# A Fourier filter and an MLP-mixer block on one core: weight loads held back for a moment, and the second group's inputs also in the filter's buffers

## The chip, the core and the metric

The kernel runs on one core of a Trainium2 chip. The core has a matmul engine (TensorE, "PE" in the profile, with its weight loads shown apart as "PEld"), VectorE ("DVE"), ScalarE ("ACT"), GpSimd ("POOL") and SyncE ("SP"). Each engine takes its own instructions strictly in the order in which the program lists them, and waits where one of them needs something that another engine or a transfer has not yet delivered. Three of them also issue DMAs: SP, ACT and POOL. A DMA behind a waiting instruction on its queue is not issued before that instruction is through. The metric is the device time of one execution in microseconds (us).

## The reference, cut to what matters

```python
X = np.fft.rfft(x, axis=1)                       # x: (8, 3008, 256) float32
Y = X * (filt_r + 1j * filt_i)[None]             # filters: (1505, 256)
y = np.fft.irfft(Y, n=3008, axis=1).astype(np.float32)

xt = y.transpose(0, 2, 1)                        # (8, 256, 3008)
h = np.maximum(xt @ w_tok1, 0) @ w_tok2          # 3008 -> 256 -> 3008 along the tokens
u = y + h.transpose(0, 2, 1)
h2 = np.maximum(u @ w_ch1, 0) @ w_ch2            # 256 -> 1536 -> 256 along the channels
out = (u + h2).astype(np.float32)
```

The weights of the mixer come in as 64-bit floats.

## The kernel before

**The filter.** The transform of length 3008 = 47 x 64 is done in steps. `a_unit` (line 462) multiplies one input tile of 2 token rows by a 64-point table; a batch has 12 units. For batches 1 to 7 ScalarE copies the result to a `t1` tile and stores it to DRAM (`z_tmp`). `b_unit` and `bi_unit` (lines 518 and 542) then go over 32 values of k: load the rows of `z_tmp`, multiply by a table, multiply by the filter on VectorE, multiply back, and store to DRAM (`g_tmp`). `t4_load` (line 594) reads `g_tmp` back in another layout. The filter rows lie in three tiles `filts`, cleared once at the start (line 924), and refilled in turn by `filt_load`, whose DMAs leave the padding rows alone. Batches go through the filter in the groups (0), (1, 2), (3, 4), (5, 6), (7).

**The inputs.** `x_load` (line 442) puts one unit, 256 KB in two DMAs, into a tile. Batch 0 uses six tile pools that are not needed yet. All later batches have the pool `xp` with XB = 2 tiles, loaded through SP: a new load can begin when the matmul on the tile before it has been done. `dft` is a generator: each `yield` is a place where the caller can put other work.

**The mixer.** `token_sums` (line 599) multiplies 24 token rows by `w1`, 96 matmul instructions (an fp32 product is two of them). `u_unit` and `u_quarter` multiply by `w2` and add the filtered input. `mix` (line 832) runs over items: 8 batches x 6 blocks of 512 tokens x 6 pairs of channel tiles, so 36 items a batch. One item is `up_first`, a ScalarE copy and two VectorE steps (`up_middle`), `up_last`, and the `down` products of the item before. Its places are numbered in the order 3, 0, 1, 2, and at each the main loop may advance the filter of the next group. For the second group (batches 1 and 2, during the items of batch 0) it advances at every place while there are `a_unit`s left (`spread`), and then 35 times over 48 places 1 and 2, that is over 24 items; for later groups at place 1 alone. The `t4` loads of batch 1 are emitted when that filter has ended, and `token_sums(1)` stands in item 32 of batch 0.

**The weights.** 38 tiles of 64-bit weights are brought to fp32. A tile has four steps, each a `yield`: its DMA (`begin`), one ScalarE activation on line 261 (`copy`), two VectorE operations on lines 263 and 264 (`middle`), and two on lines 267 and 269 (`end`). Tiles 0 to 11 are `w1`, 12 to 25 are `w2` (seven for each half; tiles 18 and 25 have 188 columns, the others 471), 26 to 37 the channel weights. Where the halves are added: for `w1` and the first BY_PE = 8 tiles of `w2` TensorE adds them (lines 302 and 303) and ScalarE copies the sum (line 305); for the rest VectorE adds them (line 291). For channel weights GpSimd then forms sums (`combine`, line 353). `convert` is `middle` and then `end` of the next tile in each iterator's turn, and after each `end` `copies` and `fill` let the next activation and the next DMAs go: a DMA is begun up to five tiles ahead of the last ended one, four among the last ten. Tiles 12 to 37 load through POOL.

**The prologue.** Lines 922 to 974: batch 0 goes through the filter (33 values of k, of which the last only finishes) while 16 tiles are converted, one half of a conversion at each k. At the last k a `middle` is called too, so from there on `middle` is one tile ahead of `end`. The rows of `g_tmp` are read back in four parts; the last one, 16 partitions, follows the last store. Then come the loads of the first two inputs of the second group, ten conversions with `token_sums(0)` after the one of tile 19, two more with the two `u_unit`s, and two `a_unit`s. All `w2` tiles are needed by the first `u_unit`, since each holds some of every block's columns. The ten remaining tiles are converted in the first five items, two in each, by half conversions (`late_half`, line 843).

Of the kernel before, what the change touches and what calls it, by code (L numbers as in the profile page):

```python
# [30 lines left out]
TC4 = 4  # L31
FB = 3
XB = 2
KC = 2
WC = 2
DT = 256
# [8 lines left out]
NG = 10  # L45
W2G = -(-N2 // NG)
PARTS = (0, 64, 96, 112)
BY_PE = 8
IN_B = 16
EARLY = 12  # L50
GROUPS = ((0,), (1, 2), (3, 4), (5, 6), (7,))
# [75 lines left out]
def kernel(  # L127
# [297 lines left out]
            advance(copy)  # L425
            copied[0] += 1

    begun = [0]

    def fill(ahead):  # L430
        while begun[0] < len(tiles) and begun[0] < ended[0] + (4 if begun[0] >= len(tiles) - len(LAST) else ahead):
            start()

    def start():
# [2 lines left out]

    xs = {}  # L440

    def x_load(b, c):

        where, tag = ((xp, "x"), (tp, "t"), (vp, "v"), (up, "u"), (t1p, "t1"), (t2p, "t2"))[c // 2] if b == 0 else (xp, "x")
        xc, dc = (2 * XC, D // 2) if b == 0 else (XC, D)
        d0, c = divmod(c, A // xc)
        t = where.tile([P, xc, dc], FP32, tag=tag, name="x")
        rows = x[b].rearrange("(n2 n1) d -> n2 n1 d", n1=N1)[:, :, ds(d0 * dc, dc)]
        for h in range(2):
            n = xc - 1 if h and (c + 1) * xc == A else xc  # L450
            lo = h * A + c * xc
            q = nc.gpsimd if b == 0 and h else nc.sync
            q.dma_start(t[h * HALF:(h + 1) * HALF, 0:n, :], rows[:, lo:lo + n, :])
            if n < xc:

                q.dma_start(t[h * HALF:(h + 1) * HALF, n:xc, :], rows[:, lo:lo + 1, :])
        xs[b, c + d0 * (A // xc)] = t
# [15 lines left out]
    def dft(bs):  # L473
# [13 lines left out]
            table_load(c)  # L487
            filt_load(c, first)

        ahead = NXC if first else XB  # L490
        for u in todo[0:ahead]:
            x_load(*u)
        if not first:
            yield True
        for i, u in enumerate(todo):
            if first and i in (0, 2):
                w_load(i // 2)
            if first and i in (6, 8):
                table_load(i // 2 - 1)
            a_unit(*u)  # L500
            if i + ahead < len(todo):
                x_load(*todo[i + ahead])
            yield i + 1 < len(todo)
            if first and (i + 1) % (NXC // 2) == 0:

                for d in range(i // (NXC // 2) * P, (i + 1) // (NXC // 2) * P, 16):
                    v = turned.rearrange("p s d -> p d s")[:, d:d + 16, :]
                    nc.vector.transpose(v, v)
# [33 lines left out]
        def bi_unit(k):  # L542
# [14 lines left out]
            if r == KC - 1:  # L557
                t3 = t3s.pop(c)
                for i, b in enumerate(bs):
                    nc.scalar.dma_start(g_d[b, ts(c, KC)].rearrange("k r d -> r k d"), t3[:, :, i, :])  # L560

        for c in range(2):
            t2_load(c)
            if not first:
                w_load(c)
# [25 lines left out]

    t4 = {}

    def t4_load(b, c, lo=PARTS[0], hi=P):
        if lo == 0:
            t4[b, c] = t4p.tile([P, TC4, D], FP32, tag="t4", name="t4")
        nc.sync.dma_start(t4[b, c][lo:hi], rows_of(g_d, b)[lo:hi, ts(c, TC4), :])

    def token_sums(b):
        acc = bank(free_bank()).rearrange("p (t d) -> p t d", t=TC)  # L600
# [231 lines left out]
    def mix(next_ready):  # L832

        wait = []
        pos, hhs, tts = {}, {}, {}

        def loads(b):
            if b + 1 < B and next_ready(b):
                for c in wait:
                    t4_load(b + 1, c)  # L840
                wait.clear()

        def late_half(f):
            if ended[0] < len(tiles):
                f()


        own = ({(3, 2): 0, (4, 2): 1}, {(2, 2): 0, (3, 0): 1, (3, 2): 2, (4, 0): 3})
        new = {(JP - 3, 2): 0, (JP - 2, 0): 1, (JP - 2, 2): 2, (JP - 1, 0): 3}

        def u_parts(b, m, jp, place):
            parts = own[b > 0] if m + 1 < MT else new if b + 1 < B else {}
            part = parts.get((jp, place))
            if part is None:
                return
            b, m = (b, m + 1) if m + 1 < MT else (b + 1, 0)
            u_part(b, m, part)
            if part == len(parts) - 1:
                if m:
                    wait.append(m)  # L860
                todo_v.extend(v_steps(b, m))
                if b and (b, m) < (B - 1, MT - 2):
                    w2m_load((m + 2) % MT)

        to_dram = [f for m in range(MT) for f in w2_sums(m)]
        items = [(b, m, jp) for b in range(B) for m in range(MT) for jp in range(JP)]
        n = MT * JP
        for i in range(len(items) + 1):
            now, old = i < len(items), i >= 1
            if now:  # L870
                b, m, jp = items[i]
                if i % n == 0:
                    wait.append(0)
                w = width(m)
                hhs[i] = hp.tile([P, 4, 256], FP32, tag="hh", name="hh")
                g = [bank("pg").rearrange("p (s n) -> p s n", s=2) for _ in range(2)]
                s = up_first(jp, uts[b, m], vts[b, m], w, g)
                up_middle(hhs[i], w, g, s)
                late_half(convert_middle)
                yield b, i % n, 3  # L880
            one_step()
            if old:
                bo, mo, jo = items[i - 1]
                tts[i - 1] = tp.tile([P, 4, 256], FP32, tag="t", name="t")
                for f in h_sums(hhs[i - 1], tts[i - 1], width(mo)):
                    f()
                down(mo, jo, 0, hhs[i - 1], tts[i - 1], pos.setdefault((bo, mo), []))
            if now:
                u_parts(b, m, jp, 0)
            late_half(convert_end)  # L890
            yield b, i % n, 0
            late_half(convert_middle)
            if now:
                up_last(jp, uts[b, m], vts[b, m], w, g, s, hhs[i])
            late_half(convert_end)
            one_step()
            loads(b)
            yield b, i % n, 1
            if old:
                down(mo, jo, 1, hhs.pop(i - 1), tts.pop(i - 1), pos[bo, mo])  # L900
                if jo == JP - 1:
                    todo_v.extend(finish(bo, mo, uts[bo, mo], pos[bo, mo]))
                    one_step()
                    one_step()
            if now:
                if b + 1 < B and i % n == n - 4:
                    h1s[b + 1] = token_relu(b + 1, token_sums(b + 1))
                u_parts(b, m, jp, 2)
                if jp == JP - 1:
                    while todo_v and m + 1 == MT:  # L910
                        one_step()
                if i >= 8 and to_dram:
                    to_dram.pop(0)()
                if i in (28, 29):
                    w2m_load(i - 28)
            loads(b)
            yield b, i % n, 2
        while todo_v:
            one_step()

    with tc.manual_schedule():
# [6 lines left out]
        for i, _ in enumerate(dft(GROUPS[0])):  # L928
            if i == 0:
                nc.scalar.dma_start(wai_t, wait_d)  # L930
            k = i - NXC - 2

            if i < NXC:
                if i in (1, 3, 5, 7, 9):
                    start()
                if i == NXC - 1:
                    copies()
                    for t, src in ((wa, wa_d), (wai, wai_d), (ident, ident_d)):
                        nc.scalar.dma_start(t, src)
            elif k >= 0:  # L940
                while half < 2 * IN_B * (k + 1) // K2:
                    if half % 2:
                        convert_end()
                    else:
                        convert_middle()
                    half += 1

                if 19 <= k < 25:
                    t4_load(0, k - 19, 0, PARTS[1])
                elif 26 <= k < 29:  # L950
                    for c in range(2):
                        t4_load(0, 2 * (k - 26) + c, PARTS[1], PARTS[2])
                elif k in (30, 31):
                    for c in range(3):
                        t4_load(0, 3 * (k - 30) + c, PARTS[2], PARTS[3])
        for c in range(A // TC4):
            t4_load(0, c, PARTS[3], P)
        both = wcp.tile([P, 2, JP, 7, P], FP32, tag="wc", name="wc")

        chan.extend((both[:, 0], both[:, 1]))  # L960
# [1 line left out]
        for i in range(IN_B, A // 2 + TC * W2G):  # L962
            convert()
            if i == A // 2 + BY_PE - 1:
                sum_up()
                acc = token_sums(0)
        h1s[0] = token_relu(0, acc)
        for dh in range(DH):
            convert()
# [13 lines left out]
        for b, i, place in mix(next_ready):  # L983
# [6 lines left out]
            due = place == 1  # L990
            if group == 0:
                due = spread
                if not spread and place in (1, 2):
                    at += 1
                    due = at * left // places > (at - 1) * left // places or at > places
            if due and not done:
# [32 lines left out]
```

## Time and profile before

| | |
|---|---|
| time, median of 5 runs | 2584.14 us (2576.14 to 2587.73) |
| the profiled execution's own time | 2586.17 us |
| its span | 2584.4 us |
| PE busy | 2495.0 us (97%) |
| PEld busy | 2052.2 us (79%) |
| DVE busy | 1912.8 us (74%) |
| ACT busy | 680.9 us (26%) |
| POOL busy | 575.8 us (22%) |
| moved by DMA | 248.37 MB, mean 96 GB/s |
| `token_sums(0)` begins | 124.9 us |
| first `u_unit` begins | 146.4 us |
| first item's ScalarE copy (line 729) | 154.8 us |
| the second group's last `a_unit` | 232.7 us |
| `token_sums(1)` begins | 495.9 us |

The profile is of one execution, and its spans are counted from the first instruction. Where an engine waits, the profile names what ended the wait; the chain of waits goes back from the last instruction to whatever released it, step by step. PE's busy time counts a matmul from its start to its modelled end, so neighbouring matmuls overlap, and a busy PE may still run below its peak rate.

### The profile page before, as it was taken

The numbers are of one execution on the slowest core, as the hardware profiler recorded it, in microseconds if no ns is written. First come the engines' busy times: TensorE is split into PE (matmuls) and PEld (weight loads), VectorE is DVE, ScalarE is ACT, GpSimd is POOL, SyncE is SP. The second block draws the span as 40 slices with busy tenths as digits, with TensorE's granted clock in tenths as the row PEclk, the third lists the DMA queues.
The fourth block names the chain that finished last, engine by engine and source line by source line (L and its number), as shares of the span: only waits on it lengthen the run. The fifth ranks groups of instructions, "written<-read, shape, count | busy, mean of one in ns | idle before, by whom it ended". The sixth has DMA issues, their size and how long they took to land.

```text
span 2584.4 us, 32295 instructions
## 1 busy us (share of the span) xinstructions
PE 2495.0 (97%) x11212; PEld 2052.2 (79%) x11212; DVE 1912.8 (74%) x3591; ACT 680.9 (26%) x1345; POOL 575.8 (22%) x1055
## 2 busy tenths in 40 slices
PE   6879999999999999999999999999999999999998
PEld 3556666888888777898888777798888888898887
DVE  6667888576686998756676899856788587757776
ACT  5623222123221222212221222212222122212222
POOL 5542232311211112112121111121121121211222
PEclk9999999999999999999999999999999999999999
DMA  9964344323342333213333333213333222111100
GB/s 216 233 186 149 116 127 146 96 93 104 103 124 78 97 104 82 92 48 103 119 109 90 89 100 112 85 37 103 102 95 107 63 79 71 39 31 36 44 13 20
DMA packets 166816, 248.37 MB, mean 96 GB/s; under 512 B 35300, under 2 KB 112474, under 8 KB 166654
## 3 DMA queue, kind: packets, MB, share of 16 engines
q1 hardware_dynamic: 94062, 152.01, 19.8%
q0 software_dynamic: 32640, 46.70, 7.3%
q10 hardware_dynamic: 39952, 47.61, 5.8%
q8 instruction: 89, 1.46, 0.2%
q14 instruction: 73, 0.60, 0.1%
HBM read 168.96 MB, written 77.22 MB: 95 GB/s over the span
## 4 chain that ended last, share of the span: by engine, by line
PE 74%; DVE 15%; DMA 5%; issue 2%; ACT 2%; POOL 0%; SPq 0%; ACTq 0%; DVEq 0%; POOLq 0%
PE ps_po L760 25%; PE ps_pg L726 15%; PE ps_pg L742 11%; PE ps_acc L603 3%; PE ps_b L603 3%; DVE t L704 3%; DVE hh L704 3%; PE ps_b L647 2%; PE ps_acc L647 2%; DVE u L704 2%; DVE s L704 2%; PE ps_b L625 2%; DMA x<-in_x_dram 2%; PE ps_acc L625 2%; PE ps_acc L524 1%
## 5 line engine op out<-in xcount | busy, mean ns | idle before, releaser
L805 POOL DMA_DIRECT2D out_dram<-r x757 | 410.5, 551 | 1778.1 <-ACT t L555 735.7
L704 DVE TENSOR_TENSOR hh<-ps_pg,s 128x512 f32<-128x512 f32 (+3 forms) x864 | 482.8, 586 | 368.4 <-ACT s L729 349.8
L747 ACT ACTIVATE hh<-hh 128x512 f32<-128x512 f32 (+1 forms) x576 | 347.8, 621 | 1191.4 <-DVE hh L704 1191.4
L760 PE MATMUL ps_po<-t,wc 128*128 128x256 f32 (+1 forms) x2304 | 537.5, 376 | 7.3 <-DVE t L704 6.4
L760 PEld LDWEIGHTS ps_po<-t,wc 128*128 128x128 f32 x2304 | 435.1, 190 | 132.3 <-issue 52.5
L726 PE MATMUL ps_pg<-v,wc 128*128 128x256 f32 (+1 forms) x1728 | 413.5, 375 | 2.4 <-DVE v L704 2.4
L760 PE MATMUL ps_po<-hh,wc 128*128 128x256 f32 (+1 forms) x1728 | 413.7, 376 | 0.2 <-ACT hh L747 0.2
L726 PEld LDWEIGHTS ps_pg<-v,wc 128*128 128x128 f32 x1728 | 327.9, 190 | 42.6 <-DVE v L704 5.5
L760 PEld LDWEIGHTS ps_po<-hh,wc 128*128 128x128 f32 x1728 | 328.9, 190 | 40.6 <-issue 2.2
L742 PE MATMUL ps_pg<-u,wc 128*128 128x256 f32 (+1 forms) x1152 | 293.9, 378 | 3.5 <-DVE hh L704 3.5
L704 DVE TENSOR_TENSOR t<-t,hh 128x256 f32<-128x256 f32 (+1 forms) x576 | 244.7, 425 | 19.9
L742 PEld LDWEIGHTS ps_pg<-u,wc 128*128 128x128 f32 x1152 | 217.0, 190 | 38.1 <-DVE hh L704 10.8
L704 DVE TENSOR_TENSOR s<-ps_pg,hh 128x512 f32<-128x512 f32 (+1 forms) x288 | 196.0, 681 | 30.7 <-DVE hh L704 0.9
L704 DVE TENSOR_TENSOR t<-hh 128x512 f32<-128x512 f32 (+1 forms) x288 | 192.3, 668 | 0.6 <-ACT hh L747 0.6
L729 ACT COPY s<-ps_pg 128x256 f32<-128x256 f32 (+1 forms) x288 | 106.0, 368 | 315.9 <-PE ps_pg L726 305.2
L742 PE MATMUL ps_pg<-v,wc 128*128 128x256 f32 (+1 forms) x576 | 169.2, 375 | 0.0
L726 PE MATMUL ps_pg<-u,wc 128*128 128x256 f32 (+1 forms) x576 | 169.2, 375 | 0.0
L726 PEld LDWEIGHTS ps_pg<-u,wc 128*128 128x128 f32 x576 | 109.5, 190 | 23.6 <-issue 11.3
L742 PEld LDWEIGHTS ps_pg<-v,wc 128*128 128x128 f32 x576 | 109.0, 190 | 13.2
L704 DVE TENSOR_TENSOR u<-ps_b,u 128x512 f32<-128x512 f32 (+3 forms) x105 | 61.1, 582 | 76.8 <-PE ps_b L647 60.3
L704 DVE TENSOR_TENSOR u<-ps_acc,u 128x256 f32<-128x256 f32 (+3 forms) x105 | 59.4, 566 | 61.3 <-PE ps_acc L647 42.4
L603 PE MATMUL ps_acc<-t,w 128*128 128x256 f32 x384 | 83.7, 380 | 1.1 <-ACT t L555 1.1
(125 smaller groups left out, 2532.0 us busy)
## 6 DMA issues: line engine op xcount, KB each, us to landing
w<-w_tmp SPq DMA_DIRECT2D x35, 896.0 KB
g_tmp<-t ACTq DMA_DIRECT2D x128, 192.0 KB
out_dram<-r POOLq DMA_DIRECT2D x698, 32.0 KB, 1.8
x<-in_x_dram SPq DMA_DIRECT2D x173, 128.0 KB
z_tmp<-t ACTq DMA_DIRECT2D x84, 256.0 KB
t<-z_tmp SPq DMA_DIRECT2D x112, 192.0 KB
t<-g_tmp SPq DMA_DIRECT2D x42, 512.0 KB
wb<-wbi_t SPq DMA_DIRECT2D x80, 224.0 KB
```

The lines of the kernel that those rows point to most:

```text
L524: nc.tensor.matmul(ps, wbs[k // WC][0:P if first else KR, k % WC, 0:P], t2, start=True, stop=True)
L603: nc.tensor.matmul(acc[:, t, :], w1[:, a, ts(t, P)], t4[b, a // TC4][:, a % TC4, :], start=(a == 0 and t == 0), stop=(a == A - 1 and t == ...
L625: nc.tensor.matmul(ps[:, ds(q * P, n)], t4[b, c][:, r, ts(dh, P)], wai[:, 0:n], start=(first and q == 0), stop=(not first and q == 3))
L647: nc.tensor.matmul(ps[:, ds(j * hw, hw)], h1[:, n, :], w2m[m % 2][:, at, 0:hw], start=(i < 2 and j == 0), stop=(j == len(todo) - 1))
L704: nc.vector.tensor_tensor(out=out, in0=in0, in1=in1, op=op)
L726: nc.tensor.matmul(ps[:, 0:hw], chan[0][:, jp, n, :], mov, start=True, stop=True)
L729: nc.scalar.copy(out=s[:, 0], in_=g[0][:, 0, 0:hw])
L742: nc.tensor.matmul(ps[:, 0:hw], chan[0][:, jp, n, :], mov, start=True, stop=True)
L747: nc.scalar.activation(out=hs, in_=hs, func=AF.Relu)
L760: nc.tensor.matmul(po[i][:, j, 0:hw], chan[1][:, jp, n, :], mov, start=(jp == 0 and first == 1), stop=(jp == JP - 1 and last == 1))
L805: q.dma_start(rows[g, e, :, ds(h * A + 4 * m, n)], blocks[ts(g, CW), h, e, 0:n])
```

## The change

The prologue and the first items are rearranged.

1. From k = 27 of the prologue's filter on, `fill` begins no new weight loads (`pause`), until the last part of the `t4` loads of batch 0 has been emitted. These six loads alternate between SP and POOL.
2. BY_PE goes from 8 to 6: tiles 18 and 19 are added on VectorE, and `token_sums(0)` stands after the conversion of tile 17 instead of 19.
3. The second group's inputs use eight buffers in turn: the two of `xp` and six halves of the three `filts` tiles. Six loads, 12 DMAs, are emitted through POOL after the prologue's conversions; each `a_unit` then emits the load that is next. When the inputs are done, GpSimd clears the three `filts` tiles before the filter rows go into them.
4. An item has three places instead of four (place 3 is gone), so that the second group gets three units an item. The conversions in the first five items are whole ones, before `up_first` and before `up_last`.

```diff
+XF = 2 * FB
-BY_PE = 8
+BY_PE = 6
...
-    begun = [0]
+    begun, pause = [0], []
     def fill(ahead):
-        while begun[0] < len(tiles) and ...
+        while not pause and begun[0] < len(tiles) and ...
...
-    def x_load(b, c):
+    def x_load(b, c, i, queue=None):
...
-        t = where.tile([P, xc, dc], FP32, tag=tag, name="x")
+        j = i % (XB + XF) - XB
+        if b in GROUPS[1] and j >= 0:
+            t = filts[j // 2][:, j % 2]
+        else:
+            t = where.tile([P, xc, dc], FP32, tag=tag, name="x")
...
-            q = nc.gpsimd if b == 0 and h else nc.sync
+            q = queue or (nc.gpsimd if b == 0 and h else nc.sync)
...
+        def more(n, queue=None):
+            for i, u in to_load[0:n]:
+                x_load(*u, i, queue)
+            del to_load[0:n]
+        more(NXC if first else XB)
+        if bs == GROUPS[1]:
+            ahead.append(more)
...
             a_unit(*u)
-            if i + ahead < len(todo):
-                x_load(*todo[i + ahead])
+            more(1)
...
+        if bs == GROUPS[1]:
+            for t in filts:
+                nc.gpsimd.memset(t, 0.0)
...
+            if ended[0] < len(tiles):
+                convert()
             if now:
...
-                late_half(convert_middle)
-                yield b, i % n, 3
...
-            late_half(convert_end)
             yield b, i % n, 0
-            late_half(convert_middle)
+            if ended[0] < len(tiles):
+                convert()
             if now:
                 up_last(jp, uts[b, m], vts[b, m], w, g, s, hhs[i])
-            late_half(convert_end)
...
+                if k == K2 - 5:
+                    pause.append(True)
...
         for c in range(A // TC4):
-            t4_load(0, c, PARTS[3], P)
+            t4_load(0, c, PARTS[3], P, (nc.sync, nc.gpsimd)[c % 2])
+        pause.clear()
...
             if i == A // 2 + BY_PE - 1:
                 sum_up()
                 acc = token_sums(0)
+        ahead[0](XF, nc.gpsimd)
         h1s[0] = token_relu(0, acc)
```

More of the change, by code (lines that the diff above doesn't have):

```diff
@@ L426, in copies @@
             copied[0] += 1
-    begun = [0]
+    begun, pause = [0], []
     def fill(ahead):
-        while begun[0] < len(tiles) and begun[0] < ended[0] + (4 if begun[0] >= len(tiles) - len(LAST) else ahead):
+        while not pause and begun[0] < len(tiles) and begun[0] < ended[0] + (4 if begun[0] >= len(tiles) - len(LAST) else ahead):
             start()
@@ L436, in start @@
         begun[0] += 1
-    xs = {}
-    def x_load(b, c):
+    xs, ahead = {}, []
+    def x_load(b, c, i, queue=None):
         where, tag = ((xp, "x"), (tp, "t"), (vp, "v"), (up, "u"), (t1p, "t1"), (t2p, "t2"))[c // 2] if b == 0 else (xp, "x")
@@ L488, in w_load @@
             filt_load(c, first)
-        ahead = NXC if first else XB
-        for u in todo[0:ahead]:
-            x_load(*u)
+        to_load = list(enumerate(todo))
+        def more(n, queue=None):
[5 more added lines that the diff above has]
+            ahead.append(more)
         if not first:
@@ L592, with t4_load @@
     t4 = {}
-    def t4_load(b, c, lo=PARTS[0], hi=P):
+    def t4_load(b, c, lo=PARTS[0], hi=P, queue=nc.sync):
         if lo == 0:
             t4[b, c] = t4p.tile([P, TC4, D], FP32, tag="t4", name="t4")
-        nc.sync.dma_start(t4[b, c][lo:hi], rows_of(g_d, b)[lo:hi, ts(c, TC4), :])
+        queue.dma_start(t4[b, c][lo:hi], rows_of(g_d, b)[lo:hi, ts(c, TC4), :])
     def token_sums(b):
@@ L841, in loads @@
                 wait.clear()
-        def late_half(f):
-            if ended[0] < len(tiles):
-                f()
         own = ({(3, 2): 0, (4, 2): 1}, {(2, 2): 0, (3, 0): 1, (3, 2): 2, (4, 0): 3})
@@ L992 @@
                 due = spread
-                if not spread and place in (1, 2):
+                if not spread and place:
                     at += 1
```

## The prediction

> **What bounds the kernel now.** I read the page first, to see which engine is full and in which slices it is not.
>
> ```profile
> PE 2495.0 (97%) x11212; PEld 2052.2 (79%) x11212; DVE 1912.8 (74%) x3591; ACT 680.9 (26%) x1345; POOL 575.8 (22%) x1055
> ...
> PE   6879999999999999999999999999999999999998
> PEld 3556666888888777898888777798888888898887
> ```
>
> Here PE's own row says little, since it is nearly full everywhere; the loads' row shows that the first seven slices (64.6 us each) are thinner than the rest. From about 520 us on PE is packed, the code there does not change, and whatever is won or lost earlier passes to the end one for one. So I went to the chain of waits for the first 500 us.
>
> ```profile
> 125.03 20.73 PE ps_b L603 x96
> ...
> 153.32 4.12 DMA x<-in_x_dram
> ...
> 164.84 6.61 DMA x<-in_x_dram
> ...
> 201.33 5.85 DMA x<-in_x_dram
> ...
> 229.25 3.29 DMA x<-in_x_dram
> ```
>
> Eight input loads lie on the chain between 153 and 233 us, 36.3 us together: with two buffers each unit waits for a load's latency. The timeline around the end of the prologue shows the other place.
>
> ```profile
> 105.44 1.15 POOL L336 DMA_DIRECT2D st<-in_moe_w_tok_dram  x2
> ...
> 115.39 0.31 ACTq L560 DMA_DIRECT2D g_tmp<-t  x1
> ...
> 119.88 2.62 SPq L597 DMA_DIRECT2D t<-g_tmp  x6
> ...
> 128.61 0.65 ACT L261 ACTIVATE both<-st 128x471 f32<-128x471 f32 x1 [2.10 <-DMA st<-in_moe_w_tok_dram]
> ...
> 131.38 0.65 ACT L261 ACTIVATE both<-st 128x471 f32<-128x471 f32 x1 [2.12 <-DMA st<-in_moe_w_tok_dram]
> ...
> 171.54 2.04 PE L464 MATMUL ps_acc<-x,wa 128*128 128x512 f32 x2 [3.94 <-DMA x<-in_x_dram]
> ```
>
> To be seen: tiles 18 and 19 are loaded at 105.4; the last `g_tmp` store is issued at 115.4 and has landed at 119.9, when SP's last loads go; tiles 23 and 24 land 2.77 us apart, late; and after 3.94 us of idleness a pair of matmuls takes 2.04 us (its neighbours 1.02 to 1.10).
>
> **Inputs: the gain.** One ScalarE copy on line 729 marks each item: 154.84 for item 0, 243.79 for item 7, 473.67 for item 29, 491.63 for item 32. I compare item 0's copy to item 32's, 336.8 us before. Prices from the timeline: an item has 28 matmul instructions, eight of 256 columns per 1.73 us, so 6.05; an `a_unit` 0.87; a `u_unit` 1.72 + 0.89 = 2.61. VectorE in an item with two conversions: 1.11 (`up_middle`) + 1.57 (`h_sums`) + 1.29 (`up_last`) + 2 x 2.95 = 9.87; its cyclic order is the same before and after, so I cost the move of the conversions at nothing but 0.2 us of waits.
>
> After, without input waits: items 0 to 2 are VectorE's, 3 x 10.1 = 30.3. Items 3 and 4 are PE's, 6.05 + 3 x 0.87 + 2.61 = 11.27, with 0.4 of waits 23.4 together. Items 5 and 6: 6.05 + 2.61 + 0.4, twice, 18.1. Together 71.8, where before has 88.95. With three units an item instead of four, the units end at item 7's first place, not item 5's, and everything behind shifts by two items: 7 and 8 are light (13.2), the 22 items with filter steps keep their 229.9 less 0.8 (one more of them is in the narrow block), and of the three items behind them (17.96) one is left (6.0). Sum 320.1: a gain of 16.7. Bounds: 22.8 if only PE's work counts; 8.5 if another wait takes 8 of it back (items 0 to 6 in 80). I take 16.7, because item 4, which waits little, took 12.8 us where the same sum with four units (6.05 + 3.48 + 2.61) gives 12.1.
>
> The 12 DMAs that move to POOL cost it 12 x 0.6 = 7 us, between the load of tile 29 and `combine` of tile 27; GpSimd would wait for VectorE there anyway (8 waits, 38.1 us, in the first 300 us). No unit needs them before about 165.
>
> **The pause and BY_PE: the loss.** The new order on the queues decides. At the pause tiles 0 to 17 have been begun. Behind it POOL has three `t4` loads, which wait for the last `g_tmp` store, then tile 18's load. ScalarE's activation of tile 18 stands ahead of its later copies, and VectorE's `middle` of 18 stands ahead of the `end` of 17, since `middle` runs one ahead. PE needs that `end` before `token_sums(0)`. So `token_sums` now waits for tile 18's load, which before came 14 us earlier. Step by step: the store lands at 118.3 (2.9 us after issue; 4.5 before, and 2.2 at the most in the last step at 472.8); three POOL issues of 0.55; tile 18 is issued at 120.05. Its landing:
>
> ```profile
> st<-in_moe_w_tok_dram POOLq DMA_DIRECT2D x2, 188.0 KB, 7.0
> ```
>
> That is the mean of two; tile 25, issued at 124.46, is activated at 133.59, so it took about 9.1 and tile 18 about 4.9. I take 4.9: landed 125.0. Activation 0.4, `middle` 0.6, `end` of 17 1.05, PE's last sum 0.95: `token_sums` begins at 128.0 instead of 124.9. PE has then idled some 7 us; behind 171.5 the slow stretch cost 1.0 + 1.2 + 0.8 = 3 us, and I add that. It ends at 151.8, relu 0.7, first `u_unit` 152.7 (146.4 before). Beside it VectorE has more to do and starts late: `middle` of 19 ends at 129.5 (landing 2.77 behind 18, activation 0.65), `end` of 18 at 130.6, 19 waits for 20's load and ends at 134.4, then 20 to 23 take 2.95 each (146.2), 24 takes 2.65 and the short 25 takes 2.15, so that the last of `w2` is done at 150.9. It is just covered. Channel tiles 26 and 27 end at 155.6, the first `combine` at 158.5, where PE, behind the `u_unit`s (5.5) and two units (1.9), is at 160.1: covered too. Loss 6.3.
>
> Bounds: the load as quick as the 224 KB stores of `w_tmp` (3.1) and no slow clock leaves `w2` at 149, a loss of 2.6; a gain is excluded because ten tiles of about 2.6 us follow tile 18 and all of `w2` stands before `u_unit`, where before VectorE was through at 140.6. With tile 25's 9.1 the loss is 10.5. The two tiles taken from PE save it 8 matmuls (3.1 us) and ScalarE two copies, off the path; VectorE's two additions (1.5 us) are in the sum. The six `t4` loads go in 1.3 us instead of 2.6, covered by the wait for tile 18.
>
> Two rules of the Trainium skill speak to this, and neither enters the sum. "DMA: Bandwidth & Descriptors", in its section on the anatomy of a GpSimd DMA, gives about 2.0 us + bytes/436 GB/s, which would be an estimate of 2.4 us for tile 18; the loss would be 3.8 and the time 2572.2. "Trainium Kernel Development and Optimization", under Key Constraints, says that queues of several engines share the same 16 DMA engines and save only the issue time: the alternation would bring nothing beyond that, and it puts three issues ahead of the weights.
>
> **Small terms.** Three GpSimd memsets (0.9 us each on VectorE at the start, so about 1 to 1.4 each) stand ahead of the filter rows, while SP waits for the last `z_tmp` store anyway; I add 1.0 (0 to 3). `token_sums(1)` now follows the filter's end by about 12 us, not 24.8. The way from the last `bi` product to the `t4` loads took 3.9 us (471.11 to 475.01) and the first 512 KB then about 4; later tiles need 2.5 and PE takes 3.45 for each. I add 0 (0 to 3).
>
> **Sum.** 2586.17 - 16.7 + 6.3 + 1.0 = 2576.8. The profiled execution lies 2.03 above the median of the runs, so against the median 2574.7.
>
> **Rivals.**
> - *Another wait takes the inputs' place.* `t1` has two buffers, so a unit's ScalarE copy waits for the `z_tmp` store two units back; this could also hold the copies that items need. For it: DMAs moved 188 GB/s over 152 to 240, and 5 us stretches reached 273, so stores may take 5 us. Against: two units are 5.5 us apart at the least. With the bound of 8.5: 2584.1 - 8.5 + 6.3 + 1.0 = 2582.9, no change.
> - *Loads set the pace of the conversions: slower.* All ten tiles from 18 on now wait in one queue, behind nothing loaded ahead. At 2.77 us a tile they just keep up with VectorE's 2.95. The second `u_unit` and item 0 slip by each excess: at 3.9 us a tile (482 KB, 124 GB/s) the slip is about 9.4 more and the gain is gone; at 4.4 it is 14, 2589. For it: tile 23 took 8.8 us from issue (119.79). Against: that pace of 2.77 already included the inputs' and `t4` loads.
> - *The pause works as a shortcut*: tile 18 lands before VectorE needs it, loss 2.6, and inputs gain 20: 2584.1 - 20 + 2.6 + 0.5 = 2567.
>
> **How the numbers follow.** 0.3%, about what a measurement of this kernel tells from no change, is 7.8 us: faster is below 2576.4. Forecast 0.5 (2568 to 2581, two thirds of it below that bound); another wait 0.2 (2576 to 2588, hardly any of it faster, 0.03); slower rival 0.12 (2584 to 2595, half of it beyond 2591.9); shortcut 0.18 (2562 to 2572). So faster 0.33 + 0.18 + 0.03 = 0.54; slower 0.06, with a little for what I have not seen 0.09; same 0.37. The range leaves out a tenth at each end: 2566 to 2589.
>
> **What the profile will show.** Right: no input on the chain in the first items, items 0 to 2 about 10 us apart, VectorE without gaps there; an idle PE of 6 to 8 us ahead of `token_sums(0)`, ended by VectorE's line 269, which follows tile 18's load; the copy of item 0 at about 161; item 32's some 320 us later. Wrong: `token_sums(0)` near 121; input or `z_tmp` waits inside items 0 to 6; a wait of PE at `token_sums(1)`; filter rows late at item 9.

## The result, and the profile after

| | before | after |
|---|---|---|
| median of the runs shown here | 2581.92 us (2573.99 to 2587.73) | 2576.85 us (2572.28 to 2581.96) |
| the profiled execution's own time | 2586.17 us | 2580.08 us |
| its span | 2584.4 us | 2578.1 us |
| last `g_tmp` store issued | 115.39 | 117.03 |
| `token_sums(0)` begins | 124.86 | 130.07 |
| first `u_unit` begins | 146.43 | 153.04 |
| item 0's ScalarE copy | 154.84 | 162.18 |
| item 32's copy | 491.63 | 484.77 |
| from item 32's copy to the span's end | 2092.7 | 2093.3 |

The ratio is 0.9982, with a 95% interval of 0.9977 to 0.9988: 4.6 us less (3.1 to 5.9; the two medians lie 5.1 apart). That is a gain, but one below the 0.3% that the prediction took as the bound: it gave 0.54 to a gain beyond that bound and 0.37 to a difference within it, so the less likely of the two came. The forecast was 2574.7, so the time itself is 2.2 us off and inside the range; the gain was forecast at 9.4 and is about half of that. The table says where it lies. The prologue ends 7.3 us later than before (162.18 against 154.84), the first 32 items take 322.6 us instead of 336.8, which is 14.2 less, and behind them both kernels need nearly the same time. The copies that mark items 0 and 32, before and then after:

```profile
154.84 0.37 ACT L729 COPY s<-ps_pg 128x256 f32<-128x256 f32 x1 [0.41 <-PE ps_pg L726]
...
491.63 0.35 ACT L729 COPY s<-ps_pg 128x224 f32<-128x224 f32 x1 [0.22 <-PE ps_pg L726]
```

```profile
162.18 0.35 ACT L743 COPY s<-ps_pg 128x256 f32<-128x256 f32 x1
...
484.77 0.35 ACT L743 COPY s<-ps_pg 128x224 f32<-128x224 f32 x1 [0.22 <-PE ps_pg L740]
```

The first rows of the page of the changed kernel, and its rows of tenths:

```profile
PE 2488.2 (97%) x11204; PEld 2048.3 (79%) x11204; DVE 1919.4 (74%) x3594; ACT 679.9 (26%) x1342; POOL 590.9 (23%) x1073
...
PE   7789999999999999999999999999999999999997
PEld 3467666888888777898888777898888888898887
```

PE has lost 8 matmuls (11204 instead of 11212) and VectorE has three instructions more. Of the slices (64.5 us each) the third, from 129 to 193 us, is fuller than before on both PE rows (8 and 6, where it was 7 and 5), and the second, the end of the prologue, is thinner (7 and 4, where it was 8 and 5).

The window from 152 to 240 us, where the input loads lay, first of before, then of after; the columns are the stretch, its length, busy time and count of PE, PEld, DVE, ACT and POOL, the granted clock, the DMA share and GB/s:

```profile
152.00:240.00 88.00, 71.57 (x242) 46.95 (x241) 53.82 (x103) 30.61 (x55) 32.56 (x62) 0.92 0.61 188
```

```profile
152.00:240.00 88.00, 75.37 (x292) 51.87 (x291) 68.01 (x123) 33.70 (x61) 49.28 (x86) 1.00 0.60 181
```

PE gets through 292 matmul instructions instead of 242 in the same 88 us, at a clock of 1.00 instead of 0.92, and no input load is left on the chain of waits there. The DMAs move no more than before (181 GB/s, before 188); the inputs are only asked for earlier. This is the gain, and its mechanism is the one that the prediction gave.

The chain of waits of the changed kernel around the end of the prologue (start, length, what):

```profile
117.03 2.13 DMA g_tmp<-t
...
121.47 4.68 DMA st<-in_moe_w_tok_dram
...
128.34 1.94 PE ps_po L304 x2
130.28 22.10 PE ps_b L617 x96
...
153.04 1.98 PE ps_acc L647 x4
```

And the same place in its timeline (start, length, engine, line, operation, out<-in, count, and in brackets the idle time before with what ended it):

```profile
117.03 0.31 ACTq L571 DMA_DIRECT2D g_tmp<-t  x1
...
119.74 1.67 POOL L611 DMA_DIRECT2D t<-g_tmp  x3 [11.77 <-DMA g_tmp<-t]
121.47 2.71 POOL L337 DMA_DIRECT2D st<-in_moe_w_tok_dram  x5
...
126.23 0.37 ACT L262 ACTIVATE both<-st 128x188 f32<-128x188 f32 x1 [7.13 <-DMA st<-in_moe_w_tok_dram]
126.64 0.26 DVE L264 TENSOR_SCALAR both<-both 128x188 uint32<-128x188 uint32 x1 [7.39 <-ACT both L262]
127.63 0.65 DVE L270 SCALAR_TENSOR_TENSOR both<-st,both 128x471 f32<-128x471 uint32 x1
128.34 1.94 PE L304 MATMUL ps_po<-both,ident 128*128 128x471 f32 x2 [7.19 <-DVE both L270]
130.07 22.29 PE L617 MATMUL ps_b<-t,w 128*128 128x256 f32 x96
```

This is read as a domino, in which each wait passes on the one before it. POOL waits 11.77 us for the last `g_tmp` store, because its three `t4` loads stand ahead of the weights; tile 18 is therefore issued at 121.47. It arrives 4.7 us later, ScalarE has then waited 7.13 us for it, VectorE 7.39 and PE 7.19. Tile 17, which PE needs, had long been loaded; only its `end` stands behind the `middle` of tile 18. After the idleness PE's pair takes 1.94 us (about 1.06 elsewhere), and the 96 matmuls of `token_sums(0)` take 22.10 on the chain (20.73 before).

### The profile page after: what moved, and what is told of

It reads as the page before. It is cut to its first block, busy times and chain, and to the rows that moved or that the text cites. A ratio compares the mean times of both kernels' runs of the same rounds, so it can differ in the third digit from the quotient of the medians.

```text
span 2578.1 us, 32285 instructions
## 1 busy us (share of the span) xinstructions
PE 2488.2 (97%) x11204; PEld 2048.3 (79%) x11204; DVE 1919.4 (74%) x3594; ACT 679.9 (26%) x1342; POOL 590.9 (23%) x1073
## 4 chain that ended last, share of the span: by engine, by line
PE 72%; DVE 18%; DMA 3%; ACT 3%; issue 2%; ACTq 0%; POOL 0%; DVEq 0%; SPq 0%; POOLq 0%
PE ps_po L774 25%; PE ps_pg L740 15%; PE ps_pg L756 10%; PE ps_b L617 4%; DVE t L718 4%; DVE hh L718 3%; PE ps_acc L661 2%; PE ps_b L661 2%; PE ps_acc L617 2%; DVE u L718 2%; DVE s L718 2%; PE ps_acc L639 2%; PE ps_b L639 2%; PE ps_b L535 1%; PE ps_acc L560 1%
## 5 line engine op out<-in xcount | busy, mean ns | idle before, releaser
L756 PEld LDWEIGHTS ps_pg<-u,wc 128*128 128x128 f32 x1152 | 216.1, 190 | 45.2 <-DVE hh L718 20.0
L718 DVE TENSOR_TENSOR u<-ps_acc,u 128x512 f32<-128x512 f32 (+3 forms) x105 | 61.1, 582 | 76.5 <-PE ps_acc L661 60.1
L617 PE MATMUL ps_b<-t,w 128*128 128x256 f32 x480 | 106.0, 383 | 1.1 <-ACT t L566 1.1
L718 DVE TENSOR_TENSOR u<-ps_b,u 128x256 f32<-128x256 f32 (+3 forms) x105 | 59.5, 566 | 61.0 <-PE ps_b L661 42.3
## 6 DMA issues: line engine op xcount, KB each, us to landing
x<-in_x_dram SPq DMA_DIRECT2D x139, 128.0 KB
```

The source lines that it names most:

```text
L617: nc.tensor.matmul(acc[:, t, :], w1[:, a, ts(t, P)], t4[b, a // TC4][:, a % TC4, :], start=(a == 0 and t == 0), stop=(a == A - 1 and t == ...
L718: nc.vector.tensor_tensor(out=out, in0=in0, in1=in1, op=op)
L756: nc.tensor.matmul(ps[:, 0:hw], chan[0][:, jp, n, :], mov, start=True, stop=True)
```

## The experiments

All kernels here compute the whole reference, except that one (e11) does some additions more than once; none leaves work out. Lines are numbered as in the changed kernel. A single profile carries some noise: the last `g_tmp` store is issued between 111.3 and 117.0 us although the code ahead of it hardly differs, so within traces I count from that store. Between item 32's copy and the end of the span lie 2092.6 to 2094.1 us in every one of these kernels, so what is won before item 32 arrives at the end. The ratio of each experiment is against runs of the kernel before that were taken beside it.

**The pause taken out (e1).**

```diff
-                if k == K2 - 5:
-                    pause.append(True)
```

> The changed kernel without the pause. Theory A (queue order): the pause and the three t4 loads on POOL together hold tile 18's load until the last g_tmp store has landed; without the pause tiles 18 to 20 are begun before. Then token_sums(0) begins near 122 us (130 in the changed kernel), the first u_unit near 144 (153), item 0's copy near 153 (162), time about 2568. Theory B (two more tiles on VectorE make the conversions late, pause or not): item 0's copy stays at 160 to 162, time 2575 to 2577. Theory C (the pause pays, since fewer transfers run beside the last rows): the last t4 loads go later and the time is 2578 to 2580.

Measured: 2568.84 us, ratio 0.9949 (0.9935 to 0.9964), against 0.9982 (0.9977 to 0.9988) for the change: the intervals lie apart, and 8.0 us separate the medians. The same place in its timeline:

```profile
116.03 0.31 ACTq L571 DMA_DIRECT2D g_tmp<-t  x1
...
118.00 0.37 ACT L262 ACTIVATE both<-st 128x188 f32<-128x188 f32 x1
...
119.69 1.80 POOL L611 DMA_DIRECT2D t<-g_tmp  x3 [7.40 <-DMA g_tmp<-t]
121.47 2.24 POOL L337 DMA_DIRECT2D st<-in_moe_w_tok_dram  x4
121.84 2.40 PE L617 MATMUL ps_b<-t,w 128*128 128x256 f32 x10 [0.68 <-issue]
...
143.71 2.00 PE L647 MATMUL ps_acc<-w,h 128*128 128x512 f32 x4 [0.90 <-ACT h L629]
```

Tile 18 is activated at 118.00, before the store has even landed, and `token_sums(0)` follows 2.1 us behind POOL's first `t4` load instead of 10.3. Item 0's copy comes 38.2 us after the last store; it was 39.5 before and 45.2 with the change. POOL still waits for the store (7.40 us), but tiles 18 to 20 went out ahead of that wait, at 105.82 and 111.75, and only the later ones stand behind it. **No version is faster (e12, below, is equal), and it is ahead of both kernels**; it is the change less two lines.

**The pause kept, all six `t4` loads on SP (e2).**

```diff
-            t4_load(0, c, PARTS[3], P, (nc.sync, nc.gpsimd)[c % 2])
+            t4_load(0, c, PARTS[3], P)
```

> The changed kernel with the pause, but all six last t4 loads on SP. Theory A: the pause then only changes the order in which loads are listed; POOL waits for nothing and issues tile 18 right behind the filter rows, near 109 us; token_sums(0) near 122, time about 2568, like the kernel without the pause. If the pause itself were the delay, tile 18 would still be issued behind the t4 loads, near 121, and the time would stay at 2576 to 2577.

Measured: 2573.46, ratio 0.9964 (0.9951 to 0.9977). Tile 18 is issued at 105.16 here: with nothing on POOL that waits for the store, the pause delays no weight at all. The long wait for tile 18 needs both the pause and the alternation. But the 2568 that was expected did not come; e2 stays 4.6 us behind e1:

```profile
114.82 0.31 ACTq L571 DMA_DIRECT2D g_tmp<-t  x1
119.44 2.62 SPq L611 DMA_DIRECT2D t<-g_tmp  x6
123.21 3.96 PE L617 MATMUL ps_b<-t,w 128*128 128x256 f32 x10 [3.32 <-ACT both L262]
```

The store needs 4.6 us to land (3.1 in e1), the six loads go one behind the other, PE idles 3.32 us (the ScalarE operation named is of a tile that `token_sums` does not need, and ended 0.7 us earlier; what `token_sums` needs here is the `t4` tiles) and its first ten matmuls take 3.96 us instead of 2.40. Since the pause delays nothing here, the alternation is what is left to explain the 4.6 us, by the later loads and the slow restart. That is argued, not shown: the kernel with neither, at BY_PE = 6, was not run, and at BY_PE = 8 the alternation brings nothing (e8 against e3, below).

**Halves of the change: only the inputs and three places (e3), only the prologue (e4).** e3 has no pause, BY_PE = 8 and all `t4` loads on SP. e4 is the kernel before with the pause, the alternation and BY_PE = 6.

> The changed kernel with its prologue put back (no pause, BY_PE = 8, t4 loads on SP): the inputs, the clearing and the item order alone. From the traces, item 0 to item 32 took 322.6 us in the changed kernel and 336.8 before, so if that gain belongs to this part alone: item 0's copy at 155, and 14 us less than before, 2568. Theory B has 2568 to 2570. If the input's gain depends on the later start of the items (more time for the loads), some of it goes: 2571 to 2574.

> The kernel before with the prologue's part alone (pause, t4 loads on SP and POOL, BY_PE = 6). Theory A: the loss of 7.3 us seen at item 0's copy, or a little less, since no inputs load on POOL: 2587 to 2590, copy of item 0 near 162. Theory B: the same sign, smaller, 2583 to 2586. Theory C: faster than before, 2579 to 2581.

Measured: e3 2570.77, ratio 0.9958 (0.9941 to 0.9975), with items 0 to 32 in 321.6 us. e4 2584.17, ratio 1.0009 (0.9998 to 1.0020), less than the 2587 to 2590 expected from the domino alone, with items 0 to 32 in 336.4, as before. Its timeline has the same domino, without any of the new input loads:

```profile
116.68 1.67 POOL L597 DMA_DIRECT2D t<-g_tmp  x3 [13.32 <-DMA g_tmp<-t]
118.41 2.71 POOL L336 DMA_DIRECT2D st<-in_moe_w_tok_dram  x5
...
124.99 1.94 PE L303 MATMUL ps_po<-both,ident 128*128 128x471 f32 x2 [6.89 <-DVE both L269]
```

The inputs win 0.42%, the prologue loses 0.09%, which by the times alone is not clear of nothing; together 0.33%, give or take 0.2, where the change has 0.18%. No interplay of the halves is needed to explain it. The prologue's loss is 2.3 us by the times (from a gain of 0.5 to a loss of 5.2) and 5.4 in the trace, counted from the last store.

**Where TensorE adds eight tiles again, without the pause (e8).**

```diff
-BY_PE = 6
+BY_PE = 8
```

> The changed kernel without the pause and with BY_PE = 8: tiles 18 and 19 by TensorE again, the loads of the last rows still on SP and POOL. If BY_PE = 6 is worth something, then because token_sums(0) does not wait for tiles 18 and 19: it begins 2.5 to 3 us later here, the first u_unit follows it, time 2571 to 2572. If the other queue for the last rows did it, no difference to 2568.8.

Measured: 2572.97, ratio 0.9968 (0.9955 to 0.9980), 4.1 us behind e1, though the intervals overlap. `token_sums(0)` begins 6.6 us after the first `t4` load instead of 2.7, since the sums of tiles 18 and 19 stand ahead of it; PE waits 1.17 and 0.75 us for VectorE between them. So BY_PE = 6 is the likely part of the prologue that helps. The alternation is not: e8 has it and e3 does not, they differ in nothing else, and e8 is no faster (0.9968 against 0.9958).

**The items' order of before, with eight input buffers (e9).** As e1, but with four places an item and half conversions.

```diff
+                late_half(convert_middle)
+                yield b, i % n, 3
...
-                if not spread and place:
+                if not spread and place in (1, 2):
```

> The changed kernel without the pause, with the items of the kernel before: conversions in halves and four places, so four units an item. The buffers alone. If the inputs' waits are all that mattered, the order of the items is worth nothing and the time is 2567 to 2570; item 0 to item 32 in 320 to 323 us. If four units an item run into the two t1 buffers or into VectorE, 2572 or more.

Measured: 2570.80, ratio 0.9958 (0.9945 to 0.9971), with items 0 to 32 in 322.3 us (321.3 in e1). Three places instead of four are worth nothing that can be measured; the buffers are the gain. The waits do differ: on e9's chain two `z_tmp` stores stand between 150 and 240 us (6.34 and 2.00 us), on that of the changed kernel none from 155 to 240.

**The six early inputs on SP instead of POOL (e10).**

```diff
-        ahead[0](XF, nc.gpsimd)
+        ahead[0](XF)
```

> The changed kernel without the pause, and with the six early inputs loaded through SP instead of POOL. On POOL they stand behind the loads of the weights (141 to 148 us in the trace without the pause). SP waits for nothing there and issues them near 123 to 129, beside the loads of tiles 21 to 25. If queues of different engines share the same transfer engines, these tiles come later by up to 1.5 MB at about 230 GB/s, 6 us, and the first u_unit with them: 2571 to 2575. If there is room for both, 2568 to 2569.

Measured: 2572.03, ratio 0.9967 (0.9954 to 0.9979).

```profile
118.82 5.36 SPq L458 DMA_DIRECT2D filt<-in_x_dram  x7
...
141.96 1.98 PE L647 MATMUL ps_acc<-w,h 128*128 128x512 f32 x4 [3.61 <-ACT h L629]
```

SP waits for nothing and asks for the inputs from 118.8 us on, among the loads of the `w2` tiles that the first `u_unit` needs. That `u_unit` then starts 3.61 us late (0.90 in e1); the relu that the line names had been done. POOL's order, inputs behind weights, pays about 3 us by the medians; the intervals overlap.

**What bounds items 0 to 2?** They took 35.1 us (11.85, 12.08 and 11.21) where the forecast had 30.3. A part of it hangs on what the prologue leaves behind: with the same items, item 0 took 9.88 us in e1 and 12.03 in e10, and e1's three items 33.3. In the waits of the changed kernel between 152 and 240 us (who waits, for what; us in total, times, longest):

```profile
ACT t L475 <- DMA z_tmp<-t: 7.4, 3, 3.7
DVE top L264 <- ACT top L262: 7.3, 5, 2.1
```

VectorE waits 7.3 us for the activations of the conversions, which stand on ScalarE behind the units' copies. The first theory (D) was that whole conversions put VectorE in phase with ScalarE's work. Two kernels on top of e1 try it: e5 does half conversions as before, e12 lists each activation one place earlier.

```diff
                 up_middle(hhs[i], w, g, s)
+                late_half(convert_middle)
...
+            late_half(convert_end)
             yield b, i % n, 0
-            if ended[0] < len(tiles):
-                convert()
+            late_half(convert_middle)
```

> The changed kernel without the pause, and with the conversions of the first five items again in halves at the places of the kernel before (three places an item kept). Items 0 to 2 took 11.85 us each in the changed kernel where I had forecast 10.1. Theory D: the whole conversion lists the next tile's ScalarE activation too late, behind a unit's copies, and VectorE waits 1.0 to 1.5 us for it once an item; then items 0 to 4 gain about 1.3 each and the time is about 2564 (2568.8 with whole conversions). Rival E: VectorE's operations themselves are slower there (0.55 us instead of 0.42 for line 268), from GpSimd working beside it, and the wait only moves: within 1.5 of 2568.8.

Measured: 2573.45, ratio 0.9970 (0.9958 to 0.9982). Items 0 and 1 become shorter (8.5 and 10.7 us), but item 2 takes 17.2:

```profile
176.59 2.07 PE L774 MATMUL ps_po<-hh,wc 128*128 128x256 f32 x4 [8.01 <-POOL wc L361]
```

PE waits 8.01 us for GpSimd's sums, since half conversions end a tile half an item later and `combine` follows the end.

```diff
+            if i == 0:
+                convert_middle()
             if ended[0] < len(tiles):
-                convert()
+                convert_end()
...
                 up_middle(hhs[i], w, g, s)
+                if ended[0] < len(tiles):
+                    convert_middle()
```

(and likewise at `up_last`)

> The changed kernel without the pause; the ScalarE activation of the next weight tile is listed one place earlier (after up_middle and after up_last) while the VectorE steps stay where the changed kernel has them. In the run with halves items 0 and 1 took 8.5 and 10.7 us (9.9 and 12.2 with whole conversions), but PE then waited 8.0 us for GpSimd's sums of a channel tile that came half an item later. Here the sums stay early. Theory D (VectorE waits 1.0 to 1.5 us an item for that activation): items 1 to 4 shorter by about 1.2 each, 2564 to 2566. If the wait only moves to another engine: 2567 to 2570.

Measured: 2568.88, ratio 0.9948 (0.9935 to 0.9961): e1's time. VectorE's wait for the activations falls from 6.0 us in e1 to 1.0 (143 to 232 us), but item 0 to 32 still takes 321.6. For example, first a line of e1, then lines of e12:

```profile
164.27 0.43 DVE L264 TENSOR_SCALAR top<-top 128x512 uint32<-128x512 uint32 x1 [1.34 <-ACT top L262]
```

```profile
162.06 0.74 DVE L264 TENSOR_SCALAR top<-top 128x512 uint32<-128x512 uint32 x1 [0.98 <-ACT top L262]
...
195.26 1.44 PE L469 MATMUL ps_acc<-filt,wa 128*128 128x512 f32 x2 [2.19 <-ACT t L475]
```

The wait has moved: now a unit's copy on line 475 is late, and PE waits for that. Theory D falls: the wait was real, and worth nothing.

**Thirty GpSimd additions more (e11).** On top of e1, the last addition of `combine` is done four times for the ten late tiles.

```diff
         add(out=s4, in0=a12, in1=s2, op=ALU.subtract)
+        for _ in range(3 if more else 0):
+            add(out=s4, in0=a12, in1=s2, op=ALU.subtract)
```

> The changed kernel without the pause; the last operation of each of GpSimd's sums for the ten late channel tiles is done three times more (30 operations, the result is the same). Theory E (VectorE's operations take longer beside GpSimd's): more of VectorE's operations on lines 264 to 292 show 0.5 to 0.7 and 0.8 us instead of 0.42 and 0.69; items 0 to 4 longer by 2 to 5 us, 2571 to 2575, more if PE has to wait for the sums. If GpSimd does not matter to VectorE: 2568 to 2570.

Measured: 2578.26, ratio 0.9989 (0.9979 to 1.0000), 9.4 us slower than e1, and items 0 to 32 take 330.6 instead of 321.3.

```profile
181.96 2.07 PE L776 MATMUL ps_po<-hh,wc 128*128 128x256 f32 x4 [6.35 <-POOL wc L363]
```

Item 2 alone takes 17.8 us, where e1's took 11.2. GpSimd, 23% busy over the whole, is nearly critical in these first items. What bounds these three items stays open: relieving VectorE of its wait for ScalarE gained nothing, and little more on GpSimd makes PE wait, so several engines hand the same time on.

## Why the prediction was right or wrong

**The mechanism of the gain was right, its size 2.5 us too large.** The forecast had 320.1 us from item 0's copy to item 32's; the trace has 322.6. By parts: items 3 and 4 took 23.7 (forecast 23.4), 5 and 6 took 17.2 (18.1), 7 and 8 took 12.9 (13.2), 9 to 30 took 228.2 (229.1), item 31 took 5.4 (6.0). The step that failed is "items 0 to 2 are VectorE's, 3 x 10.1 = 30.3": they took 35.1. "Its cyclic order is the same before and after, so I cost the move of the conversions at nothing but 0.2 us of waits" was wrong in its cover: VectorE waited 1.0 to 1.5 us an item for ScalarE, and its operations were longer beside GpSimd's (next section but one). But e12 shows that taking the first of these away brings nothing, so the sum of VectorE's operations was not the right model of these items.

**The mechanism of the loss was right, step by step.** Forecast against trace: store landed 2.9 us after its issue against 2.2; tile 18 issued at 120.05 against 121.47 (the store went out at 117.03 rather than 115.39, which made up for the quicker landing); 4.9 us to its landing against 4.7; `token_sums(0)` at 128.0 against 130.07; first `u_unit` at 152.7 against 153.04. A loss of 6.3 was forecast at the end of it; item 0's copy shows 7.3, and 5.7 when counted from the last store. The conversions of `w2` were "just covered", as written. In this one trace the slow restart came out at 1.4 us in `token_sums(0)` and 0.9 in the pair ahead of it, against the 3 us added in the forecast.

**The load of tile 18.** It took 4.7 us from issue to activation, near the 4.9 taken from the row. The Trainium skill's "DMA: Bandwidth & Descriptors", in its section on the anatomy of a GpSimd DMA, gives about 2.0 us + bytes/436 GB/s, which would make it an estimate of 2.4 us; the trace decides. What is issued beside a load matters: in e4 tile 18, with four loads right behind it, took 4.4 us to land, and tile 25, of the same size and issued by itself, 2.7.

**Costed at nothing.** The quicker issue of the `t4` loads was put at no gain ("covered by the wait for tile 18"), and so it was, since tile 18 comes later than they do. What the prediction did not work out is that this wait needs pause and alternation as a pair, and goes when either is taken away (e1, e2). The Trainium skill's "Trainium Kernel Development and Optimization" says under Key Constraints that several queues save only the issue time. Read as a rule on bandwidth, no run here speaks against it; but a DMA that waits also holds back whatever stands behind it on its queue, and that decided 8 us here.

**The small terms.** The memsets cost nothing: the item at which the filter rows begin took 12.2 us, its counterpart before 12.5. I had put 1.0. `token_sums(1)` began at 489.1 without a wait, as costed.

**The sum.** The profiled executions differ by 6.1 us: 14.2 won in the items, 7.3 lost in the prologue and 0.6 lost behind item 32, which makes 6.3 between the spans, and 0.2 the other way around the spans. The forecast of 9.4 had the gain of the items 2.5 too high, the loss of the prologue 1.0 too low and the small losses 1.0 too high. Over all the runs the difference is 4.6 us. The forecast lies nearer to the time than to the gain because the five runs that it started from had a median 2.2 us above that of all runs of the kernel before; that part of its nearness is luck.

**The rivals.** "Another wait takes the inputs' place" was half seen. Items 0 to 6 took 76.0 us, about midway between the forecast of 71.8 and that rival's 80, and its mechanism is there: ScalarE's copies at 178.09, 187.40 and 200.41 waited 3.7, 0.9 and 2.7 us for a `z_tmp` store. PE waited for line 475's copies directly once, 1.5 us at 207.59, and no `z_tmp` store is on the chain there. How much of items 1 and 2 these waits hold was not tried with a third `t1` buffer, and stays open. "Loads set the pace" did not come: behind tile 18 ScalarE waited only once more for a weight tile before 160 us, for 0.4 us. "The pause works as a shortcut" did not come either: the changed kernel took 2576.85, not 2567, and near that time one gets by leaving the pause out (2568.84).

## What to carry to other kernels

Before a DMA that waits for something is put on a queue, list what stands behind it there and which engine's next instruction in order needs that: the loads that wait here held back no weight on SP, none that was needed soon on POOL with three more weight tiles ahead of them, and cost 8 us on POOL after a pause. A change made of several parts is worth taking apart: here two lines of it lost more than the whole of it won. And where several engines hand the same time on, the wait that the profile names can be taken away without winning anything, so a gain is counted only once the time shows it.

## What the runs showed of the hardware that I had not expected

**A store's landing goes with what loads beside it.** From the issue of the last `g_tmp` store to the first load that waits for it: 2.2 us in both kernels that let no weight load run (after, e4), 3.0 to 4.4 where POOL's waiting `t4` loads hold back the later weights (e1, e5, e8 to e12), 4.5 to 5.1 where the weights run on (before, e2, e3). These are single traces, and kernels with the same prologue spread from 3.1 to 4.4 (e1, e5), so the last two groups nearly meet. In these traces the pause brings the landing forward by 0.8 to 2.2 us beyond what the waiting `t4` loads on POOL bring by themselves, and it costs the 8 us of tile 18.

**VectorE's operations lengthen beside GpSimd's.** In the timeline of the changed kernel, VectorE's lines first, with GpSimd additions running from 165.89 and 166.91:

```profile
165.89 0.46 POOL L358 TENSOR_TENSOR wc<-wc 128x128 f32<-128x128 f32 x1
165.92 0.72 DVE L268 TENSOR_SCALAR rest<-top 128x512 uint32<-128x512 uint32 x1
166.67 0.83 DVE L270 SCALAR_TENSOR_TENSOR rest<-st,rest 128x512 f32<-128x512 uint32 x1
166.91 0.90 POOL L360 TENSOR_TENSOR wc<-wc 128x128 f32<-128x128 f32 x1
...
189.95 0.42 DVE L268 TENSOR_SCALAR rest<-top 128x512 uint32<-128x512 uint32 x1
190.41 0.69 DVE L270 SCALAR_TENSOR_TENSOR rest<-st,rest 128x512 f32<-128x512 uint32 x1
191.99 0.62 POOL L357 TENSOR_SCALAR wc<-wc 128x128 f32<-128x128 f32 x1 [5.83 <-DVE wc L292]
```

The same operation takes 0.72 beside an addition of GpSimd and 0.42 without, the next 0.83 and 0.69; some of GpSimd's additions lengthen too, here one of 0.90 against 0.46. Over 150 to 240 us the means on line 268 are 0.58 for the 7 operations that overlap one of GpSimd's and 0.42 for the others. The Trainium skill, "SBUF — State Buffer", in the section "SBUF: two separate sides", tells of a pair of ports shared by both engines, which whichever starts first, VectorE's operations with two inputs in SBUF among others, holds for the whole instruction while the other is blocked. That both lengthen agrees with this; no run here separates it from other causes. Few as these overlaps are, they are part of why VectorE's conversions of the first three items took longer than the prices that the prediction had drawn from quiet stretches; e11 does not single this out, since there PE itself waits for GpSimd's sums.
